# Block-sparse attention with a Fourier mixing MLP: key sums before the key copies, the second weight by casting DMA, and w2 pieces moved behind the norm

## The chip, the core and the metric

The kernel runs on one core of one Trainium2 chip. The metric is the device time of one execution in microseconds (us). TensorE (PE) multiplies matrices into PSUM; VectorE (DVE), ScalarE (ACT) and GpSimd (POOL) work elementwise; SyncE (SP), ScalarE and GpSimd issue DMAs.

## The reference, cut to what matters

Four batches, eight heads, 768 positions, head width 64. Each query attends to its own block of 64 keys and to the three blocks whose mean key scores highest among those that are not in its future; inside that, attention is causal. The heads side by side are `x` (768 x 512 a batch). Then

```python
k_rep = k.reshape(B, H, 12, 64, D).mean(axis=3)           # block means of the keys
gate_scores = where(causal, q @ k_rep.T, -1e9)            # top 3 blocks a query, and its own
attn = softmax(where(mask, q @ k.T / 8, -1e9)) @ v
u = x + real(fft(fft(x, axis=1), axis=2))                 # over positions, then channels
un = (u - mean(u)) / sqrt(var(u) + 1e-6)
out = u + relu(un @ w_ch1) @ w_ch2                        # 512 -> 2048 -> 512
```

## The kernel before, in words

**Attention** goes by pairs of heads, 16 in all, four to a batch, in slots `t` of a software pipeline: in slot t pair t is in stage A, pair t-1 in stage B and C, pair t-2 in the scores, pair t-3 in the values. Batch b is complete in slot 4b + 6.

- Stage A transposes q and k on TensorE (`tp`, four groups of three 128 x 128 blocks, each in one PSUM bank). VectorE copies q's to `qT` (L278). Of each of k's two banks, ScalarE makes two float16 copies, one per head, into `kI_all` (L280, L281), and after them VectorE sums each block of 64 keys (L282, into `kr`); the sums are spread over the two heads by a product with `half24` (L287). GpSimd makes `qg` of `qT` (L293).
- Stage B: `gtp` = key sums times q (L301), copied by ScalarE (`gts`, L304), transposed back (`g`, L309); VectorE adds the causal constants (`gsb`, L312), takes the eight largest of each group of 12 with twelve `max` instructions (`mx`, L320), compares with the third largest (L321) and makes the mask rows `gmp` (L324). Stage C transposes them (`gt`, L335) and copies them under q in `qg` (L337).
- Scores: twelve banks a pair (`sc`, L354, three buffers), exponentials on ScalarE (`ptl`, L361), the diagonal cut by GpSimd (L365). Values: `av` (L386), divided by the row sum on VectorE (L392, L393) into `x`; `fold_pair` adds and subtracts halves (`sd` L452, `zw` L459) for the Fourier step.

**The MLP** of a batch (`gen_mlp`): `fg` (L476 and the lines about it) from `zw`; the transform over positions (`yp`, L497 and L502) with copies `yg`, `yr` on ScalarE and VectorE; then twice three row blocks of the transform over channels (`mx_0` to `mx_5` on TensorE, L528 and L530), u on VectorE (L532), its statistics (L536, L537), `rstd` on GpSimd (L540, L542), the norm (L546), and a DMA transpose of each row block into `unT`, issued by SP (L549). After that the first layer: 16 groups `ha`, `hb` (L559, L560), with ReLU on ScalarE and VectorE (L561, L562).

The second layer of batch b (`gen_w2`, `ch_0` to `ch_5`, 16 matmuls each, L572) is cut into 24 pieces of four matmuls and run inside the MLP of batch b+1: `yield from w2(n)` runs n pieces at that place. For batch 0 there are no pieces: the iterator gives 24 bare entries of 0.86, which count in the account of the interleaver only. Of the last batch, w2 runs alone at the end. The sum with u is on VectorE (L576) and the output's write on SP (L578).

**Order.** The two generators, attention of batch b+1 and MLP of batch b, are interleaved by their shares of work done: each `yield` carries a cost, and the one that is further behind its total is next. A scheduler below then sets the order on each engine's queue; every queue is in order.

**Weights.** They come as float32. `emit_weight_load` brings 1024-column pieces of 512 KB by SP into the buffers that the hidden layer uses later (`wst`, four of them, the tags hT4_0 to hT4_3); `emit_weight_cast` makes float16 of each on GpSimd (L201). w1 is pieces 0 to 7, w2 pieces 8 to 15. The slots are

```python
W_LOAD = {1: ('fft', 0, 1, 2, 3), 3: (4, 5, 6, 7), 5: (8, 9, 10, 11), 7: (12, 13, 14, 15)}
W_CAST = {3: (0, 1, 2, 3), 5: (4, 5, 6, 7), 7: (8, 9, 10, 11), 9: (12, 13, 14, 15)}
```

v comes by DMAs that GpSimd issues and that cast to float16 on the way (L230). In slots 1 to 7 a `warm` matmul of 512 columns (L129) stands after every second piece.

Of the kernel before, what the change touches and what calls it, by code (L numbers as in the profile page):

```python
# [12 lines left out]
FP = mybir.dt.float32  # L13
# [58 lines left out]
def kernel(  # L72
# [9 lines left out]
    nc = tc.nc  # L82
# [3 lines left out]
    NB = S // 64  # L86
    NST = S // 128
# [15 lines left out]
    def pst(shape, name, dtype=FP, tag="ps", bufs=None):  # L103
        return psump.tile(shape, dtype, tag=tag, name=name, bufs=bufs)
# [7 lines left out]
    half24 = cpool.tile([128, 32], FP, tag="c_half", name="half24")  # L112
    kr16_t = [cpool.tile([128, 16], FP, tag=f"kr16_{i}", name=f"kr16_{i}") for i in range(2)]
    eps1 = cpool.tile([128, 1], FP, tag="c_eps1", name="eps1")
# [30 lines left out]
    def emit_gate_consts():  # L145
        nc.sync.dma_start(cz24, dr["cz24"].ap())
        nc.sync.dma_start(half24, dr["half24"].ap())
        for t in kr16_t:
            nc.vector.memset(t, 0.0)  # L149
        nc.gpsimd.memset(v16_all[:, :, :, 64:66], 1.0)  # L150
# [12 lines left out]
    def after(dst, src):  # L163
        nc.gpsimd.tensor_copy(out=dst, in_=src)
# [12 lines left out]
    def emit_weight_load(c):  # L177


        stg = bpool.tile([128, 1536], FP, tag=f"hT4_{c % 4}", name=f"wst_{c}")[:, 0:1024]  # L180
        wst[c] = stg
        if c < 4:
            gate_on(stg[0:1, 0:1])
        if c < 8:
            dt, hf = divmod(c, 2)
            nc.sync.dma_start(out=stg, in_=moe_w_ch1[128 * dt:128 * (dt + 1),
                                                     1024 * hf:1024 * (hf + 1)])
        else:
            it = 2 * (c - 8)
            nc.sync.dma_start(out=stg.rearrange("p (i l) -> p i l", i=2),  # L190
                              in_=moe_w_ch2[128 * it:128 * (it + 2), :]
                              .rearrange("(i p) l -> p i l", p=128))

    def emit_weight_cast(c):
        if c < 8:
            dt, hf = divmod(c, 2)
            dst = w1_sb[:, dt, 1024 * hf:1024 * (hf + 1)]
        else:
            it = 2 * (c - 8)
            dst = w2_sb[:, it:it + 2, :].rearrange("p i l -> p (i l)")  # L200
        nc.gpsimd.tensor_scalar(out=dst, in0=wst[c], scalar1=1.0, scalar2=0.0,  # L201
                                op0=mybir.AluOpType.mult, op1=mybir.AluOpType.add)

    W_LOAD = {1: ('fft', 0, 1, 2, 3), 3: (4, 5, 6, 7), 5: (8, 9, 10, 11), 7: (12, 13, 14, 15)}
    W_CAST = {3: (0, 1, 2, 3), 5: (4, 5, 6, 7), 7: (8, 9, 10, 11), 9: (12, 13, 14, 15)}
# [4 lines left out]
    attn_P = {}  # L210
# [42 lines left out]
    def gen_attention():  # L253
        P = attn_P

        def stage_A(hp):
# [7 lines left out]
            kr24 = apool.tile([128, 32], FP, tag="kr24", name=f"kr24_{hp}")  # L264
            kr12 = kr16_t[hp % 2]
            d["qt"], d["qg"], d["kI"], d["kr24"] = qt, qg, kI, kr24
            for who in range(2):
                src = qn if who == 0 else kn
                for g in range(2):
                    ps = pst([128, 3, 128], f"tp_{hp}_{who}_{g}")  # L270
                    for i in range(3):
                        st = 3 * g + i
                        nc.tensor.transpose(ps[:, i, :],
                                            src[:, st, :, :].rearrange("p h d -> p (h d)"), id32)
                    flat = ps.rearrange("p a c -> p (a c)")
                    cols = slice(384 * g, 384 * (g + 1))
                    if who == 0:
                        nc.vector.tensor_copy(out=qt[:, cols], in_=flat)  # L278
                    else:
                        nc.scalar.copy(out=kI[0][0:64, cols], in_=flat[0:64])  # L280
                        nc.scalar.copy(out=kI[1][0:64, cols], in_=flat[64:128])  # L281
                        nc.vector.tensor_reduce(  # L282
                            out=kr12[:, 6 * g:6 * g + 6],
                            in_=ps.rearrange("p a (x c) -> p a x c", x=2),
                            axis=mybir.AxisListType.X, op=mybir.AluOpType.add)
                    yield 0.33
            nc.vector.tensor_tensor(out=kr24.rearrange("p (e n) -> p e n", e=2),  # L287
                                    in0=kr12.rearrange("p (o n) -> p o n", o=1)
                                    .to_broadcast([128, 2, 16]),
                                    in1=half24.rearrange("p (e n) -> p e n", e=2),  # L290
                                    op=mybir.AluOpType.mult)
# [5 lines left out]
        def stage_B(hp):  # L297
# [19 lines left out]
            mx8 = spool.tile([128, NST, 2, 8], FP, tag="mx8", name=f"mx8_{hp}", bufs=4)  # L317
            for st in range(NST):
                for e in range(2):
                    nc.vector.max(out=mx8[:, st, e, :], in_=g4[:, st, e, 0:NB])  # L320
# [141 lines left out]
    def gen_mlp(b):  # L462
# [5 lines left out]
        def w2(n):  # L468
            yield from islice(prev, n)
# [13 lines left out]
        yield from w2(2)  # L483
# [5 lines left out]
        yield from w2(4)  # L489
# [149 lines left out]
```

## Time and profile before

| what | value |
|---|---|
| median of 3 runs | 363.17 us (362.57 to 363.66) |
| profiled execution | 360.29 us, its span 358.5 us, clock 0.940 |
| TensorE busy | 323.4 us, 90% |
| VectorE, ScalarE, GpSimd busy | 227.7, 175.8, 117.9 us |
| GpSimd's 16 weight casts | 17.1 us, from 35.4 to 95.7 us |
| HBM read, written | 28.71 MB, 6.29 MB |

The span runs from the first to the last instruction; the profiled execution's own time is 1.8 us longer. TensorE's clock is the share of full speed that was granted: at full speed matmuls of 512 columns follow each other in 0.22 us, at half in 0.43. In an instruction's row the first number is its start and the second its duration, and a bracket at the end tells how long its engine stood before it and what ended that.

### The profile page before, as it was taken

How to read it: one execution, taken by the hardware profiler on the slowest of the kernel's cores; microseconds unless marked ns; L12 is line 12 of the kernel's file. 1: busy time of each engine (PE TensorE's matmuls, PEld its weight loads, DVE VectorE, ACT ScalarE, POOL GpSimd, SP SyncE). 2: the span in 40 equal slices, each digit the busy share in tenths (PEclk: the TensorE clock that was granted, in tenths of full speed). 3: DMA queues.
4: the chain of work that ended last, by engine and by line, in shares of the span. 5: the costliest groups of instructions: out<-in, count | busy, mean ns of one | idle time of the engine just before them, and what ended most of it. 6: DMA issues, size and time to landing. Idle time of an engine off the chain costs nothing.

```text
span 358.5 us, 7035 instructions
## 1 busy us (share of the span) xinstructions
PE 323.4 (90%) x2650; PEld 197.5 (55%) x2650; DVE 227.7 (64%) x690; ACT 175.8 (49%) x363; POOL 117.9 (33%) x174
## 2 busy tenths in 40 slices
PE   5678978699499999999899999999999999599995
PEld 2346656467355665656466665656565555256442
DVE  1564987999995765579857576499673167323121
ACT  1497767578264764647266854733634130034100
POOL 2574988686743410315332312141300002000000
PEclk9698989999758999999999999999999999789999
DMA  9999999989565350354923030013300003300012
GB/s 184 181 155 276 260 274 184 299 201 259 68 142 94 56 68 0 101 71 97 148 73 24 4 22 32 31 45 60 103 2 2 29 32 102 103 2 0 29 69 79
DMA packets 96154, 35.47 MB, mean 99 GB/s; under 512 B 89224, under 2 KB 89704, under 8 KB 96120
## 3 DMA queue, kind: packets, MB, share of 16 engines
q1 hardware_dynamic: 66296, 30.65, 34.2%
q0 software_dynamic: 25120, 3.18, 14.4%
q10 hardware_dynamic: 4704, 1.18, 2.1%
q8 instruction: 21, 0.34, 0.4%
q14 instruction: 13, 0.11, 0.1%
HBM read 28.71 MB, written 6.29 MB: 98 GB/s over the span
## 4 chain that ended last, share of the span: by engine, by line
PE 63%; DVE 19%; ACT 12%; DMA 3%; issue 2%; POOL 0%; SPq 0%; ACTq 0%; DVEq 0%; POOLq 0%
ACT kI_all L281 2%; DMA qn_103<-in_q_dram 2%; ACT kI_all L280 2%; DVE sd_596 L452 1%; DVE kr_0_77 L282 1%; PE warm L129 1%; PE ch_0_3470 L572 1%; PE ch_0_2295 L572 1%; PE ch_2_3773 L572 1%; DVE x_1358 L546 1%; PE ch_5_4931 L572 1%; PE ch_5_4621 L572 1%; PE ch_5_4081 L572 1%; PE ch_4_3981 L572 1%; PE ch_2_4874 L572 1%
## 5 line engine op out<-in xcount | busy, mean ns | idle before, releaser
L354 PEld LDWEIGHTS <-kI_all 76*128 76x128 f16 x416 | 33.2, 102 | 19.7 <-issue 4.4
L559 PEld LDWEIGHTS <-w_sb 128*128 128x128 f16 x256 | 25.6, 100 | 30.4 <-issue 4.3
L230 POOL DMA_DIRECT2D v_all<-in_v_dram x32 | 27.5, 861 | 30.0 <-PE av_0_1873 L386 4.8
L560 PEld LDWEIGHTS <-w_sb 128*128 128x128 f16 x256 | 25.4, 100 | 8.4 <-issue 4.9
L540 POOL TENSOR_SCALAR rstd_3_4493<-stat_3_4492 128x3 f32<-128x3 f32 x2 | 0.5, 234 | 46.8 <-DVE stat_3_4492 L537 46.8
L561 ACT ACTIVATE hT_3_0_4640<-ha_0_4644 128x512 f16<-128x512 f32 x1 | 0.6, 597 | 22.3 <-issue 22.3
L129 PE MATMUL warm<-warm_src 128*128 128x512 f16 x26 | 11.4, 438 | 0.0
L540 POOL TENSOR_SCALAR rstd_2_3705<-stat_2_3704 128x3 f32<-128x3 f32 x2 | 0.5, 235 | 18.5 <-DVE stat_2_3704 L537 18.5
L452 DVE TENSOR_TENSOR sd_596<-x_543 128x384 f16<-128x384 f16 x8 | 5.1, 654 | 0.1
L129 PEld LDWEIGHTS <-warm_src 128*128 128x128 f16 x26 | 2.8, 106 | 3.7 <-issue 3.4
L142 PE MATMUL warmps<-warm_src 128*128 128x512 f16 x8 | 3.6, 631 | 1.3 <-DVE kr_1_78 L149 1.3
L546 DVE TENSOR_SCALAR x_543<-u_1198,stat_0_1478,rstd_0_1479 128x512 f16<-128x512 f32 x6 | 4.5, 805 | 0.2 <-POOL rstd_0_1479 L542 0.2
L546 DVE TENSOR_SCALAR x_3666<-u_4394,stat_3_4492,rstd_3_4493 128x512 f16<-128x512 f32 x6 | 2.9, 543 | 2.6 <-POOL rstd_3_4493 L542 2.6
L365 POOL TENSOR_SCALAR_AFFINE_SELECT ptl_0_2318<-ptl_0_2318 128x512 f16<-128x512 f16 (+1 forms) x2 | 1.0, 520 | 10.7 <-ACT ptl_0_2318 L361 10.7
L546 DVE TENSOR_SCALAR x_1358<-u_2289,stat_1_2535,rstd_1_2536 128x512 f16<-128x512 f32 x6 | 3.8, 671 | 0.8 <-POOL rstd_1_2536 L542 0.8
L560 PE MATMUL hb_0_4645<-unT_4491,w_sb 128*128 128x256 f16 x4 | 1.6, 406 | 2.8 <-DMA unT_4491<-x_3666 2.8
L304 ACT COPY gts_1729<-gtp_1725 96x256 f32<-96x256 f32 x1 | 0.4, 368 | 7.4 <-PE gtp_1725 L301 7.4
L508 ACT CAST yg_0_4448<-yp_0_4441 128x386 f16<-128x386 f32 x1 | 0.6, 599 | 6.9 <-PE yp_0_4441 L497 6.9
L562 DVE TENSOR_SCALAR hT_3_0_4640<-hb_0_4645 128x256 f16<-128x256 f32 x1 | 0.4, 424 | 5.6 <-PE hb_0_4645 L560 5.6
L572 PEld LDWEIGHTS <-hT_3_1_4641 128*128 128x128 f16 x24 | 2.3, 98 | 2.8
L572 PEld LDWEIGHTS <-hT_3_2_4642 128*128 128x128 f16 x24 | 2.3, 98 | 2.8
L572 PEld LDWEIGHTS <-hT_3_3_4643 128*128 128x128 f16 x24 | 2.3, 98 | 2.8
(1765 smaller groups left out, 1100.2 us busy)
## 6 DMA issues: line engine op xcount, KB each, us to landing
v_all<-in_v_dram POOLq DMA_DIRECT2D x32, 96.0 KB, 4.5
out_dram<-u_1198 SPq DMA_DIRECT2D x6, 256.0 KB, 2.1
out_dram<-u_2289 SPq DMA_DIRECT2D x6, 256.0 KB
out_dram<-u_3464 SPq DMA_DIRECT2D x6, 256.0 KB, 2.1
out_dram<-u_4394 SPq DMA_DIRECT2D x6, 256.0 KB, 2.0
fs_sb<-c_FS SPq DMA_DIRECT2D x1, 582.0 KB, 5.2
wst_177<-in_moe_w_ch_dram SPq DMA_DIRECT2D x1, 512.0 KB, 7.0
wst_180<-in_moe_w_ch_dram SPq DMA_DIRECT2D x1, 512.0 KB
```

The costliest lines, as they stand in the source:

```text
L129: nc.tensor.matmul(wt, wsrc[:, 0:128], wsrc, start=True, stop=True)
L142: nc.tensor.matmul(wps, wsrc[:, 0:128], wsrc, start=True, stop=True)
L230: nc.gpsimd.dma_start(out=v16_t[e][hp][:, :, 0:64], in_=v[b, 2 * hp + e].rearrange("(jt p) d -> p jt d", p=128))
L280: nc.scalar.copy(out=kI[0][0:64, cols], in_=flat[0:64])
L281: nc.scalar.copy(out=kI[1][0:64, cols], in_=flat[64:128])
L282: nc.vector.tensor_reduce(out=kr12[:, 6 * g:6 * g + 6], in_=ps.rearrange("p a (x c) -> p a x c", x=2), axis=mybir.AxisListType.X, op=mybir ...
L354: nc.tensor.matmul(sp[:, co:co + (a1 - a0)], kI[e][0:76, 128 * jt:128 * (jt + 1)], qg[e][0:76, a0:a1], start=True, stop=True)
L452: nc.vector.tensor_tensor(out=sd[:, sgn, :, cols], in0=x_b[:, 0:3, cols], in1=x_b[:, 3:6, cols], op=op)
L546: nc.vector.tensor_scalar(out=un16[:, st, :], in0=u_b[:, st, :], scalar1=stat6[:, st, 0:1], scalar2=rstd6[:, st:st + 1], op0=SUB, op1=mybi ...
L559: nc.tensor.matmul(ha, w1s, unT[dt][:, 0:512], start=(dt == 0), stop=(dt == NDT - 1))
L560: nc.tensor.matmul(hb, w1s, unT[dt][:, 512:768], start=(dt == 0), stop=(dt == NDT - 1))
L572: nc.tensor.matmul(cps, hT[it][:, 128 * st:128 * (st + 1)], w2_sb[:, it, :], start=(it == 0), stop=(it == NIT - 1))
```

## The change

- **Key sums.** In stage A the sums of a bank (L282 before) are issued ahead of the two ScalarE copies of the same bank. The order of access to a bank is kept by semaphores, so the copies now wait for VectorE's sum where the sum waited for the second copy. The spread over the heads (L287) covers 12 of 16 columns in tiles that are set to zero once. The branch `pairs` is never taken.
- **Maxima.** The first row block holds at most two causal blocks, so its two `max` instructions are dropped; their place in two fixed tiles holds -3e38, and nothing of the block is masked by rank.
- **Second weight.** w2 comes as four pieces of four row blocks (1 MB of float32 each) by DMAs that GpSimd issues and that cast to float16 on their way straight into `w2_sb`, in slots 7 to 10. Each is held by a 1 x 1 copy that reads the `qT` of the pair before. The eight casts of w2 on GpSimd and its eight loads on SP are gone. w1's second four pieces are loaded in slot 4 (3 before), and its casts stand in slots 4 and 7 (3 and 5 before).
- **w2 pieces.** Ahead of the transform over positions stand 1, 1, 1 and 1 pieces instead of 2, 1, 1 and 4. The four that are left run with the last `yield from w2(100)`, behind the norm. For batch 0 they are bare entries that are left out.

```diff
-        for t in kr16_t:
+        for t in mx8_t:
+            nc.vector.memset(t, -3e38)
+        for t in kr16_t + kr24_t:
             nc.vector.memset(t, 0.0)
...
     def emit_weight_load(c):
+        if c >= 8:
+            it = 4 * (c - 8)
+            after(w2_sb[0:1, it, 0:1], attn_P[c - 2]["qt"][0:1, 0:1])
+            nc.gpsimd.dma_start(out=w2_sb[:, it:it + 4, :],
+                                in_=moe_w_ch2[128 * it:128 * (it + 4), :]
+                                .rearrange("(i p) l -> p i l", p=128))
+            return
         stg = bpool.tile([128, 1536], FP, tag=f"hT4_{c % 4}", name=f"wst_{c}")[:, 0:1024]
...
-    W_LOAD = {1: ('fft', 0, 1, 2, 3), 3: (4, 5, 6, 7), 5: (8, 9, 10, 11), 7: (12, 13, 14, 15)}
-    W_CAST = {3: (0, 1, 2, 3), 5: (4, 5, 6, 7), 7: (8, 9, 10, 11), 9: (12, 13, 14, 15)}
+    W_LOAD = {1: ('fft', 0, 1, 2, 3), 4: (4, 5, 6, 7), 7: (8,), 8: (9,), 9: (10,), 10: (11,)}
+    W_CAST = {4: (0, 1, 2, 3), 7: (4, 5, 6, 7)}
...
                     else:
-                        nc.scalar.copy(out=kI[0][0:64, cols], in_=flat[0:64])
-                        nc.scalar.copy(out=kI[1][0:64, cols], in_=flat[64:128])
-                        nc.vector.tensor_reduce(
-                            out=kr12[:, 6 * g:6 * g + 6],
-                            in_=ps.rearrange("p a (x c) -> p a x c", x=2),
-                            axis=mybir.AxisListType.X, op=mybir.AluOpType.add)
+                        nc.vector.tensor_reduce(
+                            out=kr12[:, 6 * g:6 * g + 6],
+                            in_=tp.rearrange("p a (x c) -> p a x c", x=2),
+                            axis=mybir.AxisListType.X, op=mybir.AluOpType.add)
+                        nc.scalar.copy(out=put(kI[0][0:64]), in_=tp[0:64])
+                        nc.scalar.copy(out=put(kI[1][0:64]), in_=tp[64:128])
...
-            mx8 = spool.tile([128, NST, 2, 8], FP, tag="mx8", name=f"mx8_{hp}", bufs=4)
-            for st in range(NST):
+            mx8 = mx8_t[hp % 2]
+            for st in range(1, NST):
                 for e in range(2):
                     nc.vector.max(out=mx8[:, st, e, :], in_=g4[:, st, e, 0:NB])
...
-        yield from w2(2)
+        yield from w2(1)
         tt(fg[:, :, 129:256], zw[:, :, 1:128], zw[:, :, 255:128:-1], SUB)
         yield from w2(1)
         tt(fg[:, :, 257:384], zw[:, :, 257:384], zw[:, :, 511:384:-1], SUB)
         yield from w2(1)
         tt(fg[:, :, 384:511], zw[:, :, 257:384], zw[:, :, 511:384:-1], ADD)
-        yield from w2(4)
+        yield from w2(1)
```

## The prediction

> **What bounds the kernel now.** I read the page first (shares, then the forty slices), then the busy time by stages of my own choosing, then the timelines of single engines in the stages where TensorE isn't full.
>
> The page, its first line, its engine shares and two rows of the slices:
>
> ```profile
> span 358.5 us, 7035 instructions
> PE 323.4 (90%) x2650; PEld 197.5 (55%) x2650; DVE 227.7 (64%) x690; ACT 175.8 (49%) x363; POOL 117.9 (33%) x174
> ...
> PE   5678978699499999999899999999999999599995
> ...
> PEclk9698989999758999999999999999999999789999
> ```
>
> A slice is 9 us. TensorE is full from slice 12 on, with a dent at slice 35 and at the very end; before slice 12 it is uneven, and the clock row falls at slices 11 and 12 and again at 35. So the share of 90% is two things: a front of about 110 us that something else paces, and a body that TensorE paces. The busy time of each engine by stage says who:
>
> ```profile
> core 0: us, PE busy (x) PEld busy (x) DVE busy (x) ACT busy (x) POOL busy (x), PEclk, DMA share, GB/s
> ...
> 20.00:60.00 40.00, 33.53 (x358) 23.72 (x353) 29.04 (x106) 30.94 (x69) 30.73 (x44) 0.91 1.17 235
> 60.00:91.00 31.00, 26.61 (x297) 19.18 (x296) 29.56 (x96) 23.87 (x54) 21.84 (x29) 0.94 1.09 237
> 91.00:110.00 19.00, 13.91 (x83) 7.88 (x83) 17.09 (x45) 7.43 (x16) 10.43 (x14) 0.58 0.67 114
> 110.00:280.00 170.00, 167.06 (x1491) 104.34 (x1490) 117.19 (x358) 93.22 (x191) 43.05 (x64) 1.00 0.29 52
> ...
> 307.00:318.00 11.00, 7.74 (x32) 3.82 (x33) 1.62 (x4) 1.79 (x3) 0.00 (x0) 0.69 0.25 72
> ```
>
> From 60 to 110 VectorE is busy 46.65 of 50 us: it paces. From 20 to 60 nobody is full; work goes round from VectorE to TensorE to ScalarE and back. From 110 to 280 TensorE is busy 167.06 of 170 at full clock, so work taken off other engines there is worth nothing beyond 3 us. At 307 there is a hole, followed by a low clock. TensorE's timeline around it:
>
> ```profile
> 305.81 0.81 PE L572 MATMUL ch_5_4621<-w_sb,hT_2_3_4147 128*128 128x512 f16 x3
> 307.48 0.38 PE L559 MATMUL ha_0_4644<-unT_4491,w_sb 128*128 128x512 f16 x1 [0.87 <-DVE u_3464 L576]
> 310.63 0.37 PE L560 MATMUL hb_0_4645<-unT_4491,w_sb 128*128 128x256 f16 x1 [2.77 <-DMA unT_4491<-x_3666]
> 310.80 0.63 PE L559 MATMUL ha_0_4644<-unT_4491,w_sb 128*128 128x512 f16 x1
> ...
> 316.16 0.38 PE L559 MATMUL ha_2_4668<-unT_4491,w_sb 128*128 128x512 f16 x1
> ```
>
> The last piece of batch 2's second weight (ch_5) is done at 306.6; the first layer of batch 3 waits to 310.6 for the transposed norm (unT), and its matmuls then take 0.43 us apart, not 0.22, until 315.5.
>
> Two causes in the front. First, who waited for ScalarE's key copies (line 281), from that line's view:
>
> ```profile
>   DVE kr_1_78 L282: 10.2, 9
>   DVE kr_0_77 L282: 5.3, 6
> ```
>
> Second, GpSimd's weight casts (line 201) stretch VectorE's operations, seen where both timelines meet:
>
> ```profile
> 67.55 1.04 POOL L201 TENSOR_SCALAR w_sb<-wst_812 128x1024 f16<-128x1024 f32 x1
> 68.56 1.13 POOL L201 TENSOR_SCALAR w_sb<-wst_814 128x1024 f16<-128x1024 f32 x1
> ...
> 67.62 1.17 DVE L452 TENSOR_TENSOR sd_596<-x_543 128x384 f16<-128x384 f16 x1
> 68.71 1.02 DVE L287 TENSOR_TENSOR kr_6_1081<-kr_0_77,half_76 128x32 f32<-128x32 f32 x1
> ```
>
> The same sd takes 0.35 us at 69.65 and the same kr product 0.19 us at 80.96, with no cast beside them; TensorE stood 3.0 us for that kr, and ran at half pace (warm matmul 0.61 us at 70.66) until 73.5.
>
> **Part 1: w2 pieces behind the norm.** A piece is 4 matmuls, 0.86 us. Ahead of the position transform there were 2+1+1+4 = 8 pieces, now 1+1+1+1 = 4. No piece is added or lost: the four go to the drain after the norm, which then holds 8. For batch 3 the order on TensorE becomes ch_0, yp, mx_0 to mx_2, ch_1, half of ch_2, mx_3 to mx_5, the rest, and only then ha_0: 56 matmuls instead of 40 stand between mx_5 and ha_0. Everything from yp_0 to the landing of unT starts 16 matmuls, 3.45 us, earlier, if its inputs are there: fg was ready long before (VectorE was idle 2.76 us before 286.62, and TensorE took yp_0 straight after ch_1). TensorE's end of ch_5 stays, since the work before it is the same. unT lands at 310.5 - 3.45 = 307.05 instead of 310.5, the wait goes from 4.0 to 0.6 us: 3.45 us. SP's queue is no obstacle: of the output writes only that of ch_2 stands between the two groups of three transposes, as before that of ch_3 did. The clock comes on top: eight ha/hb couples at 0.64 us were run at half pace, 5.1 us; at 0.325 us (two couples take 316.81 - 316.16) it is 2.6 us. After waits of 0.87 and 1.2 us in this trace (307.48, 58.41) the pace held, after 3.0 and 4.0 it fell; a wait of 0.6 should keep it: 2.5 us. Sum of part 1: 5.9 us. Less if VectorE makes the norm later than I think: bound 2 to 6.5. In batches 1 and 2 the same move lies in the full stage: 0, bounds -1.5 to +1.5. Batch 0 has no w2 work; the pieces are bare entries in the interleaver's account, and four fewer bring its transform and norm forward against attention slots 7 and 8. Where that stage now is (91 to 110, clock 0.58, TensorE waiting 1.75 and 2.18 us for kr), it may fill gaps or push attention back on VectorE. I take 0, with bounds from 4 lost to 8 won: 19 us hold only 13.91 x 0.58 = 8.1 us of full-speed matmul.
>
> **Part 2: key sums first.** The reduce (0.56 us) and the two copies (0.47 each) of one bank still exclude each other; in the order of the changed kernel the copies wait for VectorE where the reduce waited for ScalarE. The row says that the wait is real: the first reduce begins at 10.25, when the second copy (9.74 + 0.47) ends. Taken as a wait of scheduling alone it could vanish altogether; the Trainium skill, "PSUM — Partial Sum Buffer", section "PSUM bank collisions raise a hardware error", says that any two engines on one bank and quadrant at once are an error, reads against reads included. So by the rule the wait only changes its owner, and I don't count the copies as free. VectorE's waits for those copies before 91 us are 0.90 + 0.43, 0.90 + 0.23, 0.77 + 0.17, 1.40 + 0.25 and 0.60: 5.65 us; without the rule I would count all of it. The first pair's 1.33 us count whole, since ScalarE then has nothing else to do. Of the other 4.3 I take half, 2.2, since ScalarE is busy 30.94 of 40 us from 20 to 60 and its queue is in order: behind the waiting copy stand exps, behind those the score banks (three), behind those TensorE. Later waits (112, 126) lie in the full stage: 0. Sum 3.5 us; bounds: all 5.65, or 5 lost.
>
> Beside it: ten maxima instead of twelve per pair, 0.073 us each (0.87 for 12), 0.15 per pair; four pairs lie in 60 to 110: 0.6 us. Narrower kr products and four memsets: the latter stand before 5 us, where VectorE idles 3.7 us for warmps: 0.
>
> **Part 3: second weight by casting DMA.** Gone: eight casts of about 1.04 us and eight SP issues. Added: four 1x1 copies and four issues on GpSimd's queue, at the v loads' 0.86 us each (768 pieces; these have fewer): 3.4 us. The Trainium skill, "SBUF — State Buffer", section "Who interferes with whom", speaks against this: a DMA issued by GpSimd can be starved while VectorE holds their common port; the page's example goes from about 620 to 3100 ns. By it four issues would cost some 14 us on GpSimd. The rows nearest, v loads issued at 90.66 and 95.61 amid busy VectorE, took 0.91 and 0.87, so I take the rows. Even the rule's price delays no weight: the last issue waits for qT_9 (107.2), and ch_0 first reads w2 at 139.4; a 512 KB weight load landed in 7.0 to 8.6 us, so 1 MB is some 17 at most, an estimate from those rows. What it could delay is qg (0.83) behind it; that cover is ScalarE's and TensorE's other work of the slot.
>
> Gain: the stretch of the casts at 67 to 95: sd 0.82, kr 0.83, fg 1.24 (2.77 against 3 x 0.51), the comparison 0.2, gmp 1.67 (1.97 against 0.30), x 1.26 (2.72 against 1.46), the last half by qg: 5.4 us. Loss: w1's second four casts move from 48 to 57, where they stretched 0.4 us, to about 58 to 67, at the mean of 0.54 a cast (8.7 us over 16): 1.8. Net 3.6 us of VectorE's time, two thirds on the path: 2.4; bounds 0 to 6. On SP, w1's second four loads go behind two more pairs of q and k, which then leave earlier; casts at 58 to 67 still stand 40 us ahead of ha_0 (106.9): 0.
>
> **Sum.** 5.9 + 3.5 + 0.6 + 2.4 = 12.4 us. The profiled execution took 360.29 us (span 358.5, 1.8 around it), so 347.9; the median of the runs shown is 363.17, 2.9 higher, so 350.8 us for the median.
>
> **Rivals.** (a) Tail alone: ScalarE inherits all that VectorE sheds in the front. For it: ScalarE's 30.94 of 40. 363.2 - 5.9 = 357.3. (b) More: the batch 0 rearrangement also ends the low clock at 91 to 110, 7 us beyond my sum: 344. For it: 0.58 there; against it: VectorE is at 17.09 of 19 anyway. (c) Slower: the copies in ScalarE's in-order queue wait for a loaded VectorE. At pair 8 the reduce came at 92.75 and the copies at 88.5, so a copy can be held 4 us with exps behind it. The price is that hold in each of seven slots from 20 to 91: at 1.5 us a slot 10.5 lost, against 5.9 at the end, with the other gains swallowed: 367.8. It decides from 5.9/7 = 0.84 us a slot. Against it: in the new order the copies of pairs 4 and 8 stand behind all exps of their slot. (d) The weight comes late: ch_0 would wait at 139, one for one; it needs a landing over 25 us after issue. (e) The wait at 307 stays because VectorE gives unT no earlier; front gains remain: 357.
>
> **Chances.** My sum 0.50 (346 to 355), (a) with (e) 0.23, (b) 0.12, no change 0.03, (c) with (d) 0.12. About 0.3%, 1.1 us, is what the measurement can tell from no change. Faster 0.85, same 0.03, slower 0.12. Range 343.5 to 360: it leaves out (c), no change, and a corner below.
>
> **What would show it.** Right: the wait of hb_0 on unT at the end below 1 us, the clock of the last layers 1.00; the reduce no longer waiting for ScalarE; kr at 67 to 69 at 0.2 us; first full stage beginning some 6 us earlier, near 104. Wrong: kI copies with idle time released by VectorE adding to over 6 us before 90, or TensorE waiting for w_sb at ch_0.

## The result, and the profile after

The changed kernel took 353.63 us (median of 4 runs, 351.10 to 355.26), the kernel before 363.42 (4 runs, 362.57 to 364.72); the ratio is 0.972, with a 95% interval of 0.965 to 0.979. Medians here and below are over all runs, while a ratio counts only the runs within 1.5% of the fastest of their kernel (of the 29 runs of the kernel before in each of the first two groups below that leaves 17 and 13), so the two need not agree. By the medians 9.8 us were won where 12.4 had been summed up. The profiled execution took 352.98 us, its span 351.1.

The page of the kernel after, the lines that answer to those of before:

```profile
span 351.1 us, 6970 instructions
PE 319.8 (91%) x2650; PEld 195.6 (56%) x2650; DVE 224.0 (64%) x662; ACT 177.3 (51%) x363; POOL 112.4 (32%) x174
...
PE   6779798887729999999999999999999999999995
...
PEclk9689879989967999999999999999999999999999
```

The dent at slice 35 is gone from both rows. The uneven front is still there, and now ends in a 7 and a 2 at slices 11 and 12. The busy time by stages, in the same windows as before (columns: length, then busy us of TensorE, its weight loads, VectorE, ScalarE, GpSimd, then clock, DMA share, GB/s):

```profile
core 0: us, PE busy (x) PEld busy (x) DVE busy (x) ACT busy (x) POOL busy (x), PEclk, DMA share, GB/s
...
20.00:60.00 40.00, 35.40 (x347) 23.96 (x345) 29.95 (x98) 30.20 (x68) 29.73 (x42) 0.87 1.21 236
60.00:91.00 31.00, 25.19 (x261) 16.72 (x262) 27.62 (x78) 20.90 (x46) 20.03 (x29) 0.94 0.92 140
91.00:110.00 19.00, 11.37 (x103) 7.49 (x103) 13.26 (x51) 7.66 (x16) 7.64 (x13) 0.73 0.79 109
110.00:280.00 170.00, 167.91 (x1505) 105.05 (x1503) 118.49 (x347) 97.83 (x198) 43.93 (x68) 1.00 0.32 58
...
307.00:318.00 11.00, 11.00 (x70) 6.64 (x68) 3.82 (x9) 5.37 (x9) 0.00 (x0) 1.00 0.07 25
```

At 307 to 318 TensorE is busy throughout at full clock, where it had 7.74 us at 0.69. From 60 to 110 VectorE has gone from 46.65 busy us to 40.88, and yet TensorE gets hardly more done in 91 to 110 (busy time times clock is 8.3 us, before 8.1): nobody is full there any more. TensorE's timeline at the end:

```profile
293.46 12.25 PE L586 MATMUL ch<-w_sb,hT 128*128 128x512 f16 x56
305.55 0.38 PE L573 MATMUL ha<-unT,w_sb 128*128 128x512 f16 x1
305.79 0.27 PE L574 MATMUL hb<-unT,w_sb 128*128 128x256 f16 x1
305.90 0.38 PE L573 MATMUL ha<-unT,w_sb 128*128 128x512 f16 x1
```

56 matmuls of the second weight in a row, then the first layer with no bracket, that is no wait for unT, and a couple every 0.33 us at once. From the end of ch_5 to the end of the span it was 358.5 - 306.6 = 51.9 us and is 351.1 - 305.7 = 45.4: 6.5 us. But ch_5 itself ends only 0.9 us earlier (306.6 to 305.7) in this pair of profiles. So the tail gave what was predicted, and the front much less. Who ScalarE's key copies (line 298) now wait for, from that line's view:

```profile
  DVE kr L294: 12.2, 8
  DMA kn<-in_k_dram: 5.9, 1
```

The wait has changed its owner: 12.2 us of ScalarE before the copies instead of VectorE before the sums. The longest is at pair 8, on ScalarE's and then on TensorE's timeline:

```profile
97.49 0.47 ACT L298 CAST kI_all<-tp 64x384 f16<-64x384 f32 x1 [3.45 <-DVE kr L294]
```

```profile
98.50 0.63 PE L315 MATMUL gtp<-qT,kr 128*32 128x256 f32 x6 [2.02 <-ACT kI_all L299]
102.10 0.61 PE L368 MATMUL sc<-qg,kI_all 76*128 76x128 f16 x4 [2.96 <-DVE qg L351]
104.00 1.04 PE L573 MATMUL ha<-unT,w_sb 128*128 128x512 f16 x2 [1.29 <-DMA unT<-x]
```

Ahead of pair 8's sums VectorE was doing the statistics of batch 0's second three row blocks (u and its statistics, 94.47 to 96.94), and TensorE then stood three times within six us. VectorE's operations that the casts had stretched:

```profile
60.02 2.34 DVE L473 TENSOR_TENSOR zw<-sd 128x768 f16<-128x768 f16 x2
...
66.00 0.28 DVE L301 TENSOR_TENSOR kr<-kr,half 128x24 f32<-128x24 f32 x1
...
68.06 0.63 DVE L466 TENSOR_TENSOR sd<-x 128x384 f16<-128x384 f16 x2
...
71.27 2.97 DVE L490 TENSOR_TENSOR fg<-zw 128x762 f16<-128x762 f16 x4
```

kr is back from 1.02 to 0.28 us, the two sd from 1.52 to 0.63, the four fg pieces from 3.40 to 2.97. In return the two sd and the two zw of the slot before, which now meet the moved casts of w1, take 1.27 and 2.34 where they took 0.63 and 1.47. And the start of pair 6's `gtp` is at 66.43 instead of 69.78, that of pair 7 at 83.89 instead of 82.65: 3.35 us were won by pair 6 and gone one pair later:

```profile
82.65 0.63 PE L301 MATMUL gtp_1471<-qT_7_1291,kr_7_1294 128*32 128x256 f32 x6
```

```profile
83.89 0.63 PE L315 MATMUL gtp<-qT,kr 128*32 128x256 f32 x6
```

The first line is of before, the second of after. The experiments ask where the lead goes.

### The profile page after: what moved, and what is told of

Its sections match the earlier page's. It is cut to its first block, busy times and chain, and to the rows that moved or that the text cites. A ratio compares the mean times of both kernels' runs of the same rounds, so it can differ in the third digit from the quotient of the medians.

```text
span 351.1 us, 6970 instructions
## 1 busy us (share of the span) xinstructions
PE 319.8 (91%) x2650; PEld 195.6 (56%) x2650; DVE 224.0 (64%) x662; ACT 177.3 (51%) x363; POOL 112.4 (32%) x174
## 4 chain that ended last, share of the span: by engine, by line
PE 69%; DVE 12%; ACT 8%; DMA 6%; issue 2%; POOL 1%; SPq 1%; ACTq 0%; DVEq 0%; POOLq 0%
PE ch L586 21%; PE ha L573 16%; PE hb L574 8%; PE sc L368 7%; ACT ptl L375 5%; PE av L400 4%; PE tp L276 4%; DMA kn<-in_k_dram 3%; PE yp L511 2%; DVE qg L351 2%; PE gtp L315 1%; ACT yg L522 1%; DMA qn<-in_q_dram 1%; DVE u L546 1%; PE gt L349 1%
## 5 line engine op out<-in xcount | busy, mean ns | idle before, releaser
L375 ACT ACTIVATE ptl<-sc 128x512 f16<-128x512 f32 x192 | 92.9, 552 | 39.4 <-PE sc L368 37.1
L586 PE MATMUL ch<-w_sb,hT 128*128 128x512 f16 x384 | 91.1, 379 | 0.0
L573 PE MATMUL ha<-unT,w_sb 128*128 128x512 f16 x256 | 86.9, 386 | 1.3 <-DMA unT<-x 1.3
L368 PE MATMUL sc<-qg,kI_all 76*128 76x128 f16 (+2 forms) x416 | 60.7, 259 | 12.4 <-DVE qg L351 7.0
L575 ACT ACTIVATE hT<-ha 128x512 f16<-128x512 f32 x64 | 38.2, 597 | 63.7 <-PE ha L573 42.7
L574 PE MATMUL hb<-unT,w_sb 128*128 128x256 f16 x256 | 70.3, 276 | 0.0
L586 PEld LDWEIGHTS <-hT 128*128 128x128 f16 x384 | 35.4, 97 | 38.5 <-issue 2.0
L576 DVE TENSOR_SCALAR hT<-hb 128x256 f16<-128x256 f32 x64 | 27.1, 423 | 44.4 <-PE hb L574 44.3
L379 POOL TENSOR_SCALAR_AFFINE_SELECT ptl<-ptl 128x512 f16<-128x512 f16 (+1 forms) x64 | 34.9, 563 | 62.5 <-ACT ptl L375 61.7
L400 PE MATMUL av<-v_all,ptl 128*128 128x65 f16 x672 | 27.2, 196 | 1.2 <-DVE qT L284 1.0
L298 ACT CAST kI_all<-tp 64x384 f16<-64x384 f32 x32 | 15.2, 474 | 18.3 <-DVE kr L294 12.2
L294 DVE TENSOR_REDUCE kr<-tp 128x6 f32<-128x384 f32 x32 | 17.6, 549 | 6.7 <-PE tp L276 6.1
```

What stands on the lines that cost most here:

```text
L368: nc.tensor.matmul(sp[:, co:co + (a1 - a0)], kI[e][0:76, 128 * jt:128 * (jt + 1)], qg[e][0:76, a0:a1], start=True, stop=True)
L375: nc.scalar.activation(out=pt[:, po:po + wid_bank], in_=sp, func=AF.Exp, scale=0.125)
L379: nc.gpsimd.affine_select(out=dg, in_=dg, pattern=[[0, ndiag], [1, 128]], compare_op=mybir.AluOpType.is_ge, fill=zero_fill, base=0, channe ...
L400: nc.tensor.matmul(av[:, st, 0:65], pt[:, COL[jt, st]:COL[jt, st] + 128], v16[e][:, jt, 0:65], start=(cnt == 0), stop=(cnt == 20))
L573: nc.tensor.matmul(ha, w1s, unT[dt][:, 0:512], start=(dt == 0), stop=(dt == NDT - 1))
L574: nc.tensor.matmul(hb, w1s, unT[dt][:, 512:768], start=(dt == 0), stop=(dt == NDT - 1))
```

## The experiments

The theory after this reading: the front parts do win some 4 to 6 us, and most of it is given back because batch 0's bare entries let its transform overtake the attention of pairs 7 to 9. Rivals: the copies held in ScalarE's queue take it (rival c), or the new DMAs collide with something.

Each kernel was run beside the kernel before, whose median was 361.57 us for the first group (29 runs, 356.42 to 365.72), 361.90 for the second (29 runs, 356.45 to 367.51), 363.0 for the third (11 runs, 359.96 to 367.54; another chip than the first two). In the table ch_5 is the end of the last second-weight piece of batch 2 on TensorE in the profiled execution, and "rest" the span minus that. It splits the front from the tail; one profile can lie a few us off its own median. The columns "5 to 6" and "6 to 7" are the times in us from the start of one pair's `gtp` on TensorE to that of the next, for these pairs. "Loads and slots" are the casting DMAs of w2 together with the moved slots of w1.

| kernel | group | median us (range, runs) | ratio to before, 95% | 5 to 6 | 6 to 7 | ch_5 | rest |
|---|---|---|---|---|---|---|---|
| before |  |  |  | 11.4 | 12.9 | 306.6 | 51.9 |
| after (first measurement) |  | 353.63 | 0.972 (0.965-0.979) | 9.4 | 17.5 | 305.7 | 45.4 |
| e0 after again | 2 | 353.66 (350.62-355.75, 6) | 0.983 (0.977-0.989) | 9.4 | 17.6 | 308.5 | 45.4 |
| e1 before + pieces | 1 | 358.14 (355.41-362.96, 12) | 0.994 (0.990-0.999) | 11.4 | 18.8 | 309.1 | 45.9 |
| e2 before + sums first | 1 | 364.43 (362.29-366.11, 12) | 1.012 (1.008-1.016) | 13.6 | 16.3 | 311.6 | 52.2 |
| e3 before + loads and slots | 1 | 362.21 (359.85-369.00, 12) | 1.004 (1.000-1.008) | 10.6 | 12.8 | 308.5 | 50.2 |
| e7 after - pieces | 2 | 356.48 (354.39-358.76, 12) | 0.993 (0.989-0.997) | 9.4 | 13.9 | 302.1 | 50.6 |
| e5 after - sums first | 2 | 357.33 (353.31-359.64, 12) | 0.989 (0.983-0.994) | 10.7 | 16.7 | 306.8 | 45.5 |
| e6 after - loads and slots | 2 | 357.98 (355.95-360.70, 12) | 0.996 (0.992-1.001) | 13.4 | 17.0 | 310.5 | 45.8 |
| e4 after, batch 0 as before | 1 | 349.95 (348.86-351.26, 6) | 0.971 (0.967-0.975) | 9.4 | 13.9 | 302.4 | 45.6 |
| e11 = e4 | 3 | 350.73 (347.27-352.58, 6) | 0.967 (0.961-0.973) | 9.4 | 13.9 | 304.0 | 45.6 |
| e10 before + sums first to pair 5 | 3 | 368.07 (363.30-368.50, 6) | 1.014 (1.008-1.020) | 13.9 | 16.5 | 309.5 | 51.9 |
| e8 e4 + w2 loads earlier | 3 | 348.70 (348.55-349.71, 6) | 0.964 (0.960-0.968) | 9.4 | 14.1 | 301.3 | 45.7 |
| e9 e8 + copies first from pair 8 | 3 | 350.09 (347.71-351.74, 6) | 0.968 (0.963-0.973) | 9.4 | 14.2 | 300.4 | 45.4 |

The "rest" column falls into two groups: 45.4 to 45.9 with the pieces behind the norm, 50.2 to 52.2 without. That is part 1 at the end, whatever the front does. The 1.7 us within the second group are the clock: around the wait for unT the granted clock is 0.50 for 3.4 us in e3 and e7 and for 6.8 us in before, e2 and e10.

The column "5 to 6" has four values: 11.4 with the copies first and the old slots, 10.6 to 10.7 with the copies first and the new slots, 13.4 to 13.9 with the sums first (in e10 up to pair 5) and the old slots, 9.4 with the sums first and the new slots. In "6 to 7" five kernels that bring batch 0 forward (after, e0, e1, e5, e6) take 16.7 to 18.8, the others 12.8 to 14.2, but for e2 and e10 (sums first, old slots) with 16.3 and 16.5.

The first measurement of the changed kernel (ratio 0.972) and its repetition e0 (0.983) differ by as much as several of the parts below are worth, so a part is compared within its group where that is possible.

**Each part alone (e1, e2, e3).** e1 is the kernel before with the new cut of the pieces:

```diff
-        yield from w2(2)
+        yield from w2(1)
...
-        yield from w2(4)
+        yield from w2(1)
```

> The kernel before with the w2 pieces alone moved (1, 1, 1, 1 ahead of the transform). My sum gives the end 5.9 us and everything else 0: ratio 0.984. Rival theory (the front lost again what it won, because batch 0's transform and norm now come earlier): the end still gives 6 us or more, but the first layer of batch 0 begins no earlier or later than at 107 us, and the whole is worth only 3 to 4 us (0.990). In both, the last wait for unT falls from 4 us to below 1 us and the clock of the last stage is 1.00.

The tail gained 51.9 - 45.9 = 6.0 us, and ch_5 came 2.5 us later; the median gained 3.4. Where batch 0 gives it back, on TensorE's timeline of e1:

```profile
87.89 0.63 PE L301 MATMUL gtp<-qT,kr 128*32 128x256 f32 x6 [1.92 <-DVE kr L287]
...
105.55 0.59 PE L354 MATMUL sc<-qg,kI_all 76*128 76x128 f16 x4 [3.62 <-DVE qg L337]
```

Pair 7's `gtp`, at 82.65 in the kernel before and here at 87.89, and pair 7's score banks wait for VectorE, which has batch 0's work ahead of them.

e2 is the kernel before with the sums issued ahead of the copies:

```diff
-                        nc.scalar.copy(out=kI[0][0:64, cols], in_=flat[0:64])
-                        nc.scalar.copy(out=kI[1][0:64, cols], in_=flat[64:128])
                         nc.vector.tensor_reduce(
...
+                        nc.scalar.copy(out=kI[0][0:64, cols], in_=flat[0:64])
+                        nc.scalar.copy(out=kI[1][0:64, cols], in_=flat[64:128])
```

> The kernel before with the reduce of a bank ahead of its two copies, and nothing else. My sum: 3.5 us less, ratio 0.990, with the gtp of the first pair 1.3 us earlier. Rival (ScalarE inherits the wait, in order, at the slots where VectorE is loaded): the first 66 us gain 3 us, slots 6 to 9 give it back, ratio between 0.997 and 1.003.

Alone it loses 2.9 us, which neither expectation allowed for. Up to pair 5 it is mostly 1 to 2 us ahead (`gtp` at 57.17, before 58.41; at pair 4 it is 0.8 behind), and behind from pair 6 on (70.78, before 69.78). One candidate was pair 8, on ScalarE's timeline:

```profile
97.58 0.47 ACT L284 CAST kI_all<-tp 64x384 f16<-64x384 f32 x1 [3.21 <-DVE kr L280]
100.69 0.47 ACT L284 CAST kI_all<-tp 64x384 f16<-64x384 f32 x1 [2.15 <-DVE kr L280]
```

That is rival (c) as it was written. e10 below shows that it isn't where the time goes.

e3 is the kernel before with `emit_weight_load`, `emit_weight_cast`, `W_LOAD` and `W_CAST` of the kernel after (the diff of that part is above).

> The kernel before with w2 by four casting DMAs and the slots of the changed kernel for the w1 loads and casts, and nothing else. My sum: 2.4 us less, ratio 0.993, with the VectorE rows of 67 to 96 us near their lengths without a cast (kr 0.2, gmp 0.3 us). Rival (the stretch moves to w1's later casts and the time from 67 to 96 is set by the order of VectorE's queue): within 1 us, ratio 0.997 to 1.003.

It gains nothing (0.6 us later by the medians). The front is early at first: pair 8's `gtp` is at 95.17, before at 98.15. Then the fourth load, on GpSimd's timeline, and batch 0's second three transposes, on SP's, leave together:

```profile
103.87 0.85 POOL L183 DMA_DIRECT2D w_sb<-in_moe_w_ch_dram  x1 [0.30 <-POOL w_sb L220]
```

```profile
101.01 4.17 SPq L546 DMA_TRANSPOSE unT<-x  x3
```

and TensorE's timeline shows who pays:

```profile
105.07 1.86 PE L556 MATMUL ha<-unT,w_sb 128*128 128x512 f16 x4 [1.45 <-DMA unT<-x]
109.90 1.01 PE L557 MATMUL hb<-unT,w_sb 128*128 128x256 f16 x4 [2.96 <-DMA unT<-x]
```

hb starts 109.90 - 105.18 = 4.7 us after the last transpose was issued; in the kernel before it is 109.07 - 107.69 = 1.4:

```profile
109.07 1.01 PE L560 MATMUL hb_0_1826<-unT_1477,w_sb 128*128 128x256 f16 x4 [0.30 <-DMA unT_1477<-x_543]
```

**Each part taken out of the whole (e0, e5, e6, e7).** e0 is the kernel after, unchanged.

> The changed kernel itself, as the measure for the three beside it: ratio 0.972 to the kernel before, as at the first measurement.

e5 issues the two copies ahead of the sum again (the reverse of e2's diff, in the kernel after).

> The changed kernel with the two key copies ahead of the reduce again. If the sums first are a gain here (alone they cost 1.2%, with VectorE stretched by the w2 casts and ScalarE held at pair 8), this is some 3.5 us slower than the changed kernel: 0.982 to the kernel before. If sums first cost the same 4 us in any company, this is faster than the changed kernel: 0.960.

e6 is the kernel after with the loads, casts and slots of before.

> The changed kernel with the loads, the casts and the slots of w1 and w2 as before. My step of 2.4 us for the casts taken off GpSimd says 0.979 to the kernel before. If the parts depend on each other (sums first loses through the casts' stretch), 5 us or more slower than the changed kernel: 0.986 or above. If the casting DMA is worth nothing (alone 1.004), as the changed kernel: 0.972.

e7 is the kernel after with 2, 1, 1 and 4 pieces, for all batches.

> The changed kernel with the w2 pieces at their old places for all batches (2, 1, 1, 4). The end loses its 6.5 us, batch 0's account wins back 3 to 4 us: 3 us slower than the changed kernel, 0.980 to the kernel before. If the end were worth nothing by itself, it would be 3 us faster than the changed kernel. The wait for unT at the end is 4 us and the clock after it low, as before.

By the medians, against e0's 353.66, the sums are worth 3.7 us within the whole, loads and slots 4.3, the cut of the pieces 2.8; by the ratios 2.0, 4.8 and 3.5 us of 360. The intervals of e0 and e5 overlap, so the first is soft; that of e6 lies clear of e0's, and those of e0 and e7 just touch. e5 and e7 are slower against the kernel before than the 0.982 and 0.980 expected, as e0 itself is (0.983 for 0.972); e6 came as its second expectation has it, with parts that depend on each other. The point is the contrast: alone the three parts sum to 3.4 - 2.9 - 0.6 = -0.1 us, together they win 8.2 (361.90 - 353.66). e7, which holds only the two front parts and the maxima, wins 5.4 (ch_5 at 302.1, before 306.6), where sums and loads by themselves each lose. One needs the other, and the two slot columns show some 6 us of it: sums and new slots together bring "5 to 6" from 11.4 to 9.4, where the sums alone raise it to 13.6 and the new slots alone win 0.8; in "6 to 7" the sums alone cost 3.4 us, together with the new slots 1.0. The maxima, with the narrower kr products, stand in every kernel made from the changed one and in none of e1 to e3, and no run leaves them out. e5 and e6 are 1.8 and 3.3 us faster by the medians than the parts that they hold sum to alone; how much of that belongs to the maxima is open.

e6 shows how the sums and the slots meet, on VectorE's timeline and then on TensorE's:

```profile
59.13 3.31 DVE L469 TENSOR_TENSOR sd<-x 128x384 f16<-128x384 f16 x2
62.47 0.55 DVE L354 COPY qg<-gt 12x768 f16<-12x768 f16 x1
```

```profile
63.08 2.27 PE L371 MATMUL sc<-qg,kI_all 76*128 76x128 f16 x14 [3.23 <-DVE qg L354]
```

With the sums first and the old slots, the sd of slot 5 (pair 2's) stands in the middle of w1's second four casts (55.36 to 62.23 on GpSimd) and takes 3.31 us for two. In the kernel before the last of these casts was over when sd came, and the two took 0.63:

```profile
56.58 1.04 POOL L201 TENSOR_SCALAR w_sb<-wst_421 128x1024 f16<-128x1024 f32 x1
```

```profile
58.96 0.63 DVE L452 TENSOR_TENSOR sd_596<-x_543 128x384 f16<-128x384 f16 x2
```

sd comes at the same time in both (58.96 and 59.13). It is the casts that end 4.6 us later in e6. In the kernel before two of the four stand ahead of the slot's first `qg` on GpSimd's queue; with the sums first the scheduler has put all four behind it, the last two behind a load of v each. The second qg copy on VectorE is behind sd, and TensorE waits for it. In the kernel after, w1's casts in this slot stand apart from each other, sd meets one of them (1.27 us), and the same score banks wait 0.54 us, for GpSimd.

**Does the hold at pair 8 make sums-first lose alone (e10)?** The kernel before with the sums first for pairs 0 to 5 only, the old order from pair 6 on:

```diff
-                        nc.scalar.copy(out=kI[0][0:64, cols], in_=flat[0:64])
-                        nc.scalar.copy(out=kI[1][0:64, cols], in_=flat[64:128])
+                        if hp >= 6:
+                            nc.scalar.copy(out=kI[0][0:64, cols], in_=flat[0:64])
+                            nc.scalar.copy(out=kI[1][0:64, cols], in_=flat[64:128])
                         nc.vector.tensor_reduce(
...
+                        if hp < 6:
+                            nc.scalar.copy(out=kI[0][0:64, cols], in_=flat[0:64])
+                            nc.scalar.copy(out=kI[1][0:64, cols], in_=flat[64:128])
```

> The kernel before with sums first for pairs 0 to 5 only, copies first from pair 6 on. If the loss of sums first alone (1.012) comes from slots 6 to 9, where ScalarE waited 0.5 to 3.2 us for VectorE, this is at least as fast as the kernel before: 0.990 to 0.997. If it comes from w1's casts meeting VectorE earlier in the slots, before pair 6, it stays slower: 1.005 or above.

It is still slower than before, as the second expectation has it, so sums first in slots 6 to 9 isn't needed for the loss. At pair 5 it is 3.6 us ahead (`gtp` at 54.78, before 58.41), at pair 6 only 1.1. Between them, on VectorE's and GpSimd's timelines:

```profile
56.02 2.19 DVE L456 TENSOR_TENSOR sd<-x 128x384 f16<-128x384 f16 x2
58.25 0.55 DVE L341 COPY qg<-gt 12x768 f16<-12x768 f16 x1
```

```profile
55.96 1.06 POOL L201 TENSOR_SCALAR w_sb<-wst 128x1024 f16<-128x1024 f32 x1
56.96 0.87 POOL L230 DMA_DIRECT2D v_all<-in_v_dram  x1
57.86 1.26 POOL L201 TENSOR_SCALAR w_sb<-wst 128x1024 f16<-128x1024 f32 x1
```

and on TensorE's timeline, with its busy time in a window of 58 to 68 below:

```profile
58.86 2.21 PE L358 MATMUL sc<-qg,kI_all 76*128 76x128 f16 x14 [2.16 <-DVE qg L341]
60.87 0.84 PE L273 MATMUL tp<-id,qn 128*128 128x128 f32 x3
61.51 0.63 PE L129 MATMUL warm<-warm_src 128*128 128x512 f16 x1
```

```profile
58.00:68.00 10.00, 9.01 (x82) 6.41 (x83) 6.55 (x25) 6.96 (x15) 5.93 (x8) 0.66 1.20 303
```

Here sd comes 2.9 us earlier than before and the casts end 1.5 us later (59.12, before 57.62): they meet. TensorE stands 2.16 us, and then its clock in this window is 0.66 (0.70 in e2; 1.00 in the kernel before and in the kernel after): the warm matmul takes 0.63 us and has its 0.38 again only at 66.92. VectorE's next sums (66.38) then wait 3.01 us for TensorE's transposes. So the lead is paid back by a wait and at half pace. The rest goes in the next slot, which takes 16.5 us where the kernel before takes 12.9; why, I did not follow.

**Batch 0 (e4, e11).** The kernel after, with batch 0's entries as in the kernel before:

```diff
-        yield from w2(1)
+        yield from w2(1 if b else 2)
...
-        yield from w2(1)
+        yield from w2(1 if b else 4)
```

> The changed kernel with batch 0's bare entries as before (2, 1, 1, 4), batches 1 to 3 with 1, 1, 1, 1. If bringing batch 0's transform forward costs the front some 2 us (pair 7's gtp is later in the changed kernel by 1.2 us after pair 6's was earlier by 3.4), this is 2 us faster than the changed kernel: ratio 0.967 to the kernel before. If the account of batch 0 is worth nothing, it equals the changed kernel: 0.972. If the earlier transform was a gain, it is slower: 0.978.

> The changed kernel with batch 0's bare entries as before, once more, as the measure for the two versions that start from it: some 3 us under the changed kernel's 353.7, 350.

349.95 and 350.73 us, 3 to 3.7 below the kernel after by the medians; ch_5 at 302.4 and 304.0 against 305.7 and 308.5. They weren't in one group with e0 (e11 on another chip), and the intervals of their ratios lie clear of e0's but overlap that of the first measurement, so that the size is known to a us or two only. Two comparisons inside a group agree: e1's tail gives 6.0 us and its median 3.4, so its front gives back 2.5; e7 lacks 5.1 us of tail against e0 and is only 2.8 slower, so its front is 2.3 ahead. Pair 7's `gtp` is at 80.72 (after 83.89), pair 8's at 94.25 (98.50), pair 9's at 114.24 (121.96), in e4. Slot "6 to 7" takes 13.9 us in both, against 17.5 and 17.6. Against e7, whose only difference is the pieces of batches 1 to 3, e4 is 6.5 us faster by the medians (356.48 - 349.95, two groups) and 5.0 in "rest", with ch_5 within 0.3 us: in batches 1 and 2 the move is worth nothing, as predicted.

**The loads earlier (e8), and the copies first late (e9).** e8 is e4 with all four w2 loads in slots 7 and 8:

```diff
-            after(w2_sb[0:1, it, 0:1], attn_P[c - 2]["qt"][0:1, 0:1])
+            after(w2_sb[0:1, it, 0:1], attn_P[6 + (c - 8) // 2]["qt"][0:1, 0:1])
...
-    W_LOAD = {1: ('fft', 0, 1, 2, 3), 4: (4, 5, 6, 7), 7: (8,), 8: (9,), 9: (10,), 10: (11,)}
+    W_LOAD = {1: ('fft', 0, 1, 2, 3), 4: (4, 5, 6, 7), 7: (8, 9), 8: (10, 11)}
```

> The same with the four casting DMAs of w2 in slots 7 and 8, two each. In the version it starts from, the last one is issued at 102.5 us amid the transposes of batch 0's norm, and the first layer waits 2.4 us for unT. If that collision costs the time, the wait falls to 0.3 us as in the kernel before, and the whole gains 2 to 3 us: 347.5. If the early DMAs delay q and k instead (queues are full before 85 us), it is 1 to 3 us slower: 352.

GpSimd's timeline has the last of the four loads long before the transposes, and TensorE's shows the wait:

```profile
79.06 0.76 POOL L187 DMA_DIRECT2D w_sb<-in_moe_w_ch_dram  x1
```

```profile
104.32 1.01 PE L574 MATMUL hb<-unT,w_sb 128*128 128x256 f16 x4 [0.44 <-DMA unT<-x]
```

In e4 this hb waited 2.44 us and started 2.1 us after the last transpose was issued; here it is 104.32 - 102.96 = 1.4, as in the kernel before. The collision is thus shown: with the fourth load issued among the transposes hb starts 2.1 to 2.4 us after the last issue in e4, e7 and e11, 0.7 to 1.1 more than the 1.4 without it. Why it is 3.3 more in e3 is open. e8 is 2.0 us below e11 by the medians, with overlapping intervals. It is the fastest version run: 348.70 us, below every run of the kernel before.

e9 is e8 with the copies first from pair 8 on:

```diff
+                        if hp >= 8:
+                            nc.scalar.copy(out=put(kI[0][0:64]), in_=tp[0:64])
+                            nc.scalar.copy(out=put(kI[1][0:64]), in_=tp[64:128])
                         nc.vector.tensor_reduce(
...
-                        nc.scalar.copy(out=put(kI[0][0:64]), in_=tp[0:64])
-                        nc.scalar.copy(out=put(kI[1][0:64]), in_=tp[64:128])
+                        if hp < 8:
+                            nc.scalar.copy(out=put(kI[0][0:64]), in_=tp[0:64])
+                            nc.scalar.copy(out=put(kI[1][0:64]), in_=tp[64:128])
```

> The version with w2 in slots 7 and 8, and from pair 8 on the copies ahead of the reduce again. In the version without it TensorE waits 1.1 and 1.0 us at 90 to 93 us for ScalarE's copies, which wait for VectorE. If that hold costs time, 2 us less than the version with w2 in slots 7 and 8. If VectorE paces the slot in either order, the same.

350.09 against 348.70: taking the hold at pair 8 away brings nothing, as the second expectation has it. VectorE has the same work in either order; that this is the reason is argued and not tested.

## Why the prediction was right, and where its sum was off

The direction, the range (343.5 to 360) and the working of the tail were right; the time of the likeliest case, 350.8, was 2.8 us too low. That it came so near is partly luck: in the front a cost was taken at nothing, and two gains came near their sizes for reasons that the prediction doesn't have. By its steps:

- **Part 1, the tail, 5.9 us: right.** 6.5 us in the pair of profiles, 6.0 in e1, 4.9 to 5.1 between e7 and e4 or e0. The wait of hb on unT went from 2.77 to nothing, the clock from 0.69 to 1.00. That a wait of 0.6 us keeps the pace was a thin rule: in the same trace of before the clock fell to 0.50 at 29.0 us after waits of 0.60, 0.43 and 0.60, and at 49.5 after one of 1.99. At 307 it wasn't put to the test, since in the kernel after nothing waits there; in e1 the pace held after a wait of 0.40.
- **Part 1, batch 0, taken at 0 with bounds from 4 lost to 8 won: mis-sized.** It costs 3 to 3.7 us by e4 and e11, 2.3 to 2.5 inside the groups of e0 and e1. The prediction named this mechanism ("push attention back on VectorE") and weighed it against an empty stretch at 91 to 110. But that stretch was empty because pairs 8 and 9 hung on VectorE, and four entries fewer put more of batch 0's transform and statistics ahead of them on that engine. This term is most of the shortfall: the front parts gave 5.4 (e7) where 6.5 had been summed, the tail 5 to 6, and batch 0 took 2.3 to 3.7; 8.2 was measured in that group against 12.4.
- **Part 2, sums first, 3.5: the right size in company, and by luck.** 3.7 by e5's median, 2.0 by its ratio, with overlapping intervals. The rule on which the wait only changes its owner held: 12.2 us before the copies, of which 5.4 lie before 90 us, just under the 6 that were to count as a sign of being wrong. Taken alone, the step has the wrong sign (e2, +2.9), for a reason that the prediction doesn't have. It had the casts stretch VectorE, but took GpSimd's queue as it stood; with the sums first w1's casts come later on that queue, and slot 5's sd, which they had missed, meets them.
- **Part 2, ten maxima, 0.6: not tried alone.** A pair's ten take 0.80 to 0.82 us in the trace of after, where twelve took 0.95. What they are worth in time is open.
- **Part 3, casting DMA, 2.4 (bounds 0 to 6): 4.3 within the whole, but for another reason.** The prediction counted a stretch relieved at 67 to 95 and booked the move of w1's casts as a loss of 1.8. The runs show this move to be a gain where the sums come first: e6, with the old slots, loses 4.0 us to the changed kernel between pairs 5 and 6 (13.4 against 9.4), before any cast of w2 begins. With loads and slots alone, the step is worth nothing (e3); the collision with the transposes, which the prediction doesn't have, takes part of it, but e7 has that collision too. That a busy VectorE starves the issues wasn't seen: the four took 0.76 to 0.85 us in the kernel after, so the prediction was right to take the rows. Its estimate of some 14 us for four starved issues comes out nearer 12 by its own figure (four times 3.1).
- **Rivals.** (a) Tail alone: no, e7 keeps 5.4 us without it. (b) More: no, the low clock at 91 to 110 went only from 0.58 to 0.73, and batch 0's move lost. (c) The hold is there (3.45 us at pair 8, whose copies begin at 97.49), but from 20 to 91 us the copies wait 1.5 us in all, 0.2 a slot against the 0.84 that would decide; e9 shows no price for the hold at pair 8, and e10 shows that the loss of sums alone doesn't need it. (d) The weight isn't late: in the groups of the page, the second layer has no idle time before it:

```profile
L586 PE MATMUL ch<-w_sb,hT 128*128 128x512 f16 x384 | 91.1, 379 | 0.0
```

The last two numbers are the mean duration in ns and the idle time before the group. (e) The wait at 307 did not stay.

- **"First full stage some 6 us earlier"** failed: the wrong place to look, since batch 0's first layer came 2.9 us earlier (104.00 against 106.86) only by pushing pairs 8 and 9 behind it. The stage's start says nothing if the order of the work before it has changed; the end of ch_5 did.
- **What the measurement can tell.** I took 0.3%. Within a group of 29 the kernel before ran from 356.45 to 367.51 us, about 1.5% to either side, so single runs decide nothing below that, and several of the sizes above are medians only. In such a group the longer runs mostly have the lower granted clock (0.952 in the run of 356.45, 0.933 in that of 367.51), so a part of the spread goes with TensorE's pace; whether it comes from it was not tested.

## What to carry to other kernels

Parts of a change meet each other through time: one that alters when an engine's work comes can also alter the order on another queue, and bring together two operations that had missed each other. So cost a part together with what it will then stand beside, and test it by leaving it out as well as by adding it alone. The time from one pair to the next, read in every trace, told the parts apart where medians could not. A stage that looks empty may be waiting for one engine; before moving work into it, ask which engine that is and what the moved work puts ahead on that queue. To tell front from tail in two traces, take an event on the bounding engine after which nothing differs, here the end of ch_5, and compare the two sides of it apart.

## What the runs showed of the hardware

- DMA transposes beside one casting load: from the issue of the last of three to the first matmul that reads it 1.4 us without such a load (before, e1, e6, e8, e9), 2.1 to 2.4 with one issued among them (e4, e7, e11), and 4.7 in e3.
- VectorE's sd, two SBUF inputs, is 0.63 us for two when GpSimd casts nothing, and 2.19 (e10) to 3.31 (e6) between casts. This is as the Trainium skill has it, in "SBUF — State Buffer", section "Who interferes with whom": such an instruction contends with a GpSimd instruction that reads SBUF.
- In e10 a TensorE wait of 2.16 us in an unevenly filled stretch was followed by half pace (clock 0.50) for 6.83 us, from 59.38 to 66.21; in the 3.41 us ahead of that TensorE was busy for 1.08. The Trainium skill, "TensorE: Matmul & The Clock Gate", section "What's actually happening", gives an idle window of about 3.4 us for it; here less was enough. In all the traces half pace, but for the last one at the end of the program, lasted whole multiples of 3.41 us, from 3.41 to 20.48 (e3).
